# Linear attention followed by an MLP on one core: from two phases, one after the other, to one list-scheduled pipeline over batches

## The chip, the cores and the metric

The kernel runs on one core of one Trainium2 chip. The metric is device time in microseconds (us) of the slowest core, here the only one.

In the profile PE is TensorE's matmuls, PEld its weight loads, DVE is VectorE, ACT is ScalarE, POOL is GpSimd and SP is SyncE. L252 is line 252 of the kernel in question, so the same line number means something else in another kernel.

## The reference

```python
# q, k, v: (8 batches, 8 heads, 576 tokens, 64); omega: (128, 64)
def phi(x):                                   # on q and on k, both scaled by 64 ** -0.25
    h = einsum('bhsd,md->bhsm', x, omega) - sum(x * x, -1) / 2
    return exp(h - max(h, -1)) / sqrt(128)
q_p, k_p = phi(q_s), phi(k_s)
kv  = einsum('bhsm,bhsd->bhmd', k_p, v)
z   = sum(k_p, axis=2)
x   = (q_p @ kv) / (q_p @ z + 1e-6)           # attention, linear in the number of tokens
x   = x.transpose(0, 2, 1, 3).reshape(4608, 512)
h   = x @ w_in                                # (512, 2048)
out = (h * clip(h + 3, 0, 6) / 6) @ w_out     # (2048, 512), float32
```

Inputs and output are float32; both kernels multiply in bf16. Both drop the factors of a query token, which cancel in the quotient, and turn the maximum of a key token into a factor on its row of v.

## The kernel before

It works head by head, 64 heads, with 96 tokens on the partitions and six groups of them. Each engine has its program written out in order, with one semaphore for each kind of step. When all heads are done, the whole of x is transposed, and then the MLP runs.

```python
        def pe_T(g):                       # q and k of one head: transposes of 96 columns
            ...                            # waits for both casts, and for both exps of head g-2
            for r in range(NR):            # NR = 6
                ins = PE.transpose(rb[0:2 * D, CH * r:CH * r + CH], qkb[u][:, r, :, :]..., identb[0:CH, 0:CH])
        ...
        def pe_proj(g):
            PE.wait_ge(s_evq[u].h, g // 2 + 1)
            for i, (c0, c1) in enumerate(PQC):     # query: rows 0 to 63 of the array, 2 x 288 columns
                ins = PE.matmul(reg[0:M, c0:c1], omT[0:D, :], qkT[u][0:D, SH * i:SH * i + SH])
                if i == 1:
                    s_pq[u].inc(ins)
            for r in range(2, NR):                 # key: rows 64 to 127, 6 x 128 columns
                projk(r)
            PE.wait_ge(s_pq[u].h, g // 2 + 1)      # TensorE waits for its own query projection
            projk(0)
            s_pk[u].inc(projk(1))
        ...
        for t in range(NH + 5):            # NH = 64 heads
            dma_head(t + 2)
            pe_T(t); pe_kv(t - 2); pe_num(t - 3); pe_proj(t)
            act_expk(t - 1); act_expq(t - 1); act_kvc(t - 2); act_castk(t + 1)
            dve_div(t - 4); dve_evq(t); dve_rmax(t - 1); pool_castq(t + 1)   # runs on VectorE, despite its name
            pool_cmult(t - 1)
            ...                            # bounds of t, and the loads of the weights, cut
        for b in range(B):                 # all of x, transposed for the MLP
            for j in range(NJ):
                ...
        for tb in range(NBLK):             # 9 blocks of 512 tokens
            mm1_block(tb)                  # 16 x 4 matmuls of 512 columns; relu on ScalarE, min and product on VectorE
            ...
            if tb >= 1:
                mm2_block(tb - 1)          # 4 x 16 matmuls of 512 columns; copy on ScalarE; store
```

The softmax here doesn't subtract the row's maximum and nothing guards it: scores larger than these inputs give would overflow.

Of the kernel before, what the change touches and what calls it, by code (L numbers as in the profile page):

```python
# [12 lines left out]
class _Sem:  # L13
    __slots__ = ("h", "n")

    def __init__(self, h):
        self.h = h
        self.n = 0

    def inc(self, ins, d=1):  # L20
        ins.then_inc(self.h, d)
        self.n += d
        return ins
# [17 lines left out]
def _emit(nc, es, q, k, v, omega, w_in, w_out, out):  # L41
# [4 lines left out]
    NR = 6  # L46
    CH = S // NR
    assert S == CH * NR and CH <= 96 and S % 2 == 0, "kernel assumes seq = 6*CH, CH<=96"
    assert D == 64 and 96 <= M <= 128 and omega.shape[1] == D
    assert w_in.shape[0] == HID and w_out.shape[0] == DFF and w_out.shape[1] == HID  # L50
    NTOK = B * S
    assert out.shape[0] == NTOK and out.shape[1] == HID
    assert NTOK % 128 == 0 and HID % 128 == 0 and DFF % 128 == 0
    NJ = HID // 128
    NF = DFF // 128
    NH = B * H
    BLK = 512
    NBLK = (NTOK + BLK - 1) // BLK
    alpha = float(D) ** -0.25
    DE = D + 2  # L60
    SH = S // 2

    PE, ACT, DVE, POOL, SP = nc.tensor, nc.scalar, nc.vector, nc.gpsimd, nc.sync
# [4 lines left out]
    def pst(name, shape, dt):  # L68
        return es.enter_context(nc.psum_tensor(name, list(shape), dt))

    def sem(name):
        return _Sem(es.enter_context(nc.semaphore(name)))

    qk32 = [sbt("qk32_%d" % u, [CH, NR, 2, D], F32) for u in range(2)]
    qkb = [sbt("qkb%d" % u, [CH, NR, 2, D], BF16) for u in range(2)]
    vb = [sbt("vb%d" % u, [CH, NR, DE], F32) for u in range(4)]
    vc = [sbt("vc%d" % u, [CH, NR, DE], BF16) for u in range(2)]
    qkT = [sbt("qkT%d" % u, [2 * D, S], BF16) for u in range(2)]
    qpT = [sbt("qpT%d" % u, [M, S], BF16) for u in range(4)]
    kp = [sbt("kp%d" % u, [CH, NR, M], BF16) for u in range(2)]  # L80
    mx = [sbt("mx%d" % u, [CH, NR], F32) for u in range(2)]
    cc = [sbt("cc%d" % u, [CH, NR], F32) for u in range(2)]
    rec = [sbt("rec%d" % u, [CH, NR], F32) for u in range(2)]
    kvs = [sbt("kvs%d" % u, [M, DE], BF16) for u in range(2)]
    omT = sbt("omT", [2 * D, M], BF16)
    om32 = sbt("om32", [M, D], F32)
    omb = sbt("omb", [M, D], BF16)
    ident32 = sbt("ident32", [128, 128], F32)
    identb = sbt("identb", [128, 128], BF16)
    halfc = sbt("halfc", [128, 1], F32)  # L90
    xbufs = [sbt("xb%d" % bb, [CH, NR, HID], BF16) for bb in range(B)]
    xT = [sbt("xT%d" % j, [128, NTOK], BF16) for j in range(NJ)]
    w_in_bf = sbt("w_in_bf", [128, NJ, DFF], BF16)
    w_out_bf = sbt("w_out_bf", [128, NF, HID], BF16)
    gT = [sbt("gT%d" % u, [128, NF, BLK], BF16) for u in range(2)]
    NHP = 4
    tsb = [sbt("tsb%d" % u, [128, BLK], BF16) for u in range(NHP)]
    NTC = BLK // 128
    osb = [sbt("osb%d" % u, [128, NTC, HID], F32) for u in range(2)]

    P8 = pst("p8", [128, 4096], F32)
    regs = [P8[:, 0:1536], P8[:, 1536:3072]]
    regb = [r.bitcast(BF16) for r in regs]
    numbk = [P8[:, 3072:3584], P8[:, 3584:4096]]
    PQC = [(0, SH), (512, 512 + SH)]

    def pk_cols(r):
        if r == 0:
            return (SH, SH + M)
        if r == 1:  # L110
            return (512 + SH, 512 + SH + M)
        return (1024 + M * (r - 2), 1024 + M * (r - 1))

    s_qin = [sem("qin%d" % u) for u in range(2)]
    s_kin = [sem("kin%d" % u) for u in range(2)]
    s_vin = [sem("vin%d" % u) for u in range(4)]
    s_cq = [sem("cq%d" % u) for u in range(2)]
    s_ck = [sem("ck%d" % u) for u in range(2)]
    s_tt = [sem("tt%d" % u) for u in range(2)]
    s_evq = [sem("evq%d" % u) for u in range(2)]  # L120
    s_pq = [sem("pq%d" % u) for u in range(2)]
    s_pk = [sem("pk%d" % u) for u in range(2)]
    s_mx = [sem("mx%d" % u) for u in range(2)]
    s_rmx = [sem("rmx%d" % u) for u in range(2)]
    s_eq = [sem("eq%d" % u) for u in range(2)]
    s_ek = [sem("ek%d" % u) for u in range(2)]
    s_kv = [sem("kv%d" % u) for u in range(2)]
    s_kvc = [sem("kvc%d" % u) for u in range(2)]
    s_cm = [sem("cm%d" % u) for u in range(2)]
    s_num = [sem("num%d" % u) for u in range(2)]  # L130
    s_rec = [sem("rec%d" % u) for u in range(2)]
    s_div = [sem("div%d" % u) for u in range(2)]
    s_xtp = [sem("xtp%d" % u) for u in range(2)]
    s_xev = [sem("xev%d" % u) for u in range(2)]
    s_mm1 = [sem("mm1_%d" % u) for u in range(NHP)]
    s_hs1 = [sem("hs1_%d" % u) for u in range(NHP)]
    s_hs2 = [sem("hs2_%d" % u) for u in range(NHP)]
    s_mm2 = [sem("mm2_%d" % u) for u in range(2)]
    s_oev = [sem("oev%d" % u) for u in range(2)]
    s_c0 = sem("c0")  # L140
    s_idb = sem("idb")
    s_om = sem("omdma")
    s_omc = sem("omc")
    s_omt = sem("omt")
    s_oms = sem("oms")
    s_w = sem("wdma")
    s_out = [sem("odma%d" % u) for u in range(2)]

    blk = es.enter_context(nc.Block())

    @blk.sync
    def _body(_eng):
        s_c0.inc(POOL.memset(ident32[:], 0.0))
        POOL.wait_ge(s_c0.h, s_c0.n)
        s_c0.inc(POOL.affine_select(out=ident32[:], in_=ident32[:],
                                    compare_op=ALU.not_equal, fill=1.0, base=0,
                                    pattern=[[-1, 128]], channel_multiplier=1))
        c0_ident = s_c0.n
        s_c0.inc(POOL.memset(halfc[:], 0.5))
        c0_half = s_c0.n  # L160
        for u in range(4):
            s_c0.inc(POOL.memset(vb[u][:, :, :], 0.0))  # L162
        POOL.wait_ge(s_c0.h, s_c0.n)
        for u in range(4):
            s_c0.inc(POOL.memset(vb[u][:, :, D:D + 1], 1.0))
        c0_vb = s_c0.n
        POOL.wait_ge(s_c0.h, c0_ident)
        s_idb.inc(POOL.dma_start(identb[:], ident32[:]), 16)
        w_next = [0]
        NWP = NF + DFF // 128  # L170

        s_om.inc(SP.dma_start(om32[:], omega), 16)
        ACT.wait_ge(s_om.h, 16)
        s_omc.inc(ACT.copy(omb[:], om32[:]))
        PE.wait_ge(s_omc.h, 1)
        PE.wait_ge(s_idb.h, 16)
        PE.transpose(regb[0][0:D, 0:M], omb[:], identb[0:M, 0:M])
        s_omt.inc(PE.transpose(regb[0][D:2 * D, 0:M], omb[:], identb[0:M, 0:M]))
        ACT.wait_ge(s_omt.h, s_omt.n)
        s_oms.inc(ACT.copy(omT[:, :], regb[0][0:2 * D, 0:M]))  # L180

        def head_bh(g):
            return divmod(g, H)

        def dma_head(g):
            b, h = head_bh(g)
            u = g % 2
            if g < 2:
                SP.wait_ge(s_c0.h, c0_vb)
            if g >= 2:  # L190
                SP.wait_ge(s_cq[u].h, g // 2)
                SP.wait_ge(s_ck[u].h, g // 2)
            s_qin[u].inc(SP.dma_start(
                qk32[u][:, :, 0, :], q[b, h].rearrange("(r p) d -> p r d", p=CH)), 16)
            s_kin[u].inc(SP.dma_start(  # L195
                qk32[u][:, :, 1, :], k[b, h].rearrange("(r p) d -> p r d", p=CH)), 16)
            if g >= 4:
                SP.wait_ge(s_cm[u].h, g // 2 - 1)
            s_vin[g % 4].inc(SP.dma_start(
                vb[g % 4][:, :, 0:D], v[b, h].rearrange("(r p) d -> p r d", p=CH)), 16)  # L200

        def in_val(g):
            return 16 * (g // 2 + 1)

        def pool_castq(g):
            u = g % 2
            DVE.wait_ge(s_qin[u].h, in_val(g))
            if g >= 2:
                DVE.wait_ge(s_tt[u].h, g // 2)
            s_cq[u].inc(DVE.tensor_copy(qkb[u][:, :, 0, :], qk32[u][:, :, 0, :]))  # L210

        def act_castk(g):
            u = g % 2
            ACT.wait_ge(s_kin[u].h, in_val(g))
            if g >= 2:
                ACT.wait_ge(s_tt[u].h, g // 2)
            s_ck[u].inc(ACT.copy(qkb[u][:, :, 1, :], qk32[u][:, :, 1, :]))  # L217

        def pe_T(g):
            u = g % 2  # L220
            rb = regb[u]
# [132 lines left out]
        for t in range(NH + 5):  # L354
            if t + 2 < NH:
                dma_head(t + 2)
            if t < NH:
                pe_T(t)
# [187 lines left out]
```

## Time and profile before

| | before |
|---|---|
| time, median of 2 runs | 459.48 us (459.21 to 459.74) |
| attention, all heads | to 191 us (the last numerators; the prediction took 187) |
| transposes of x | from 192 to about 203 us |
| MLP | the remaining 254 us |
| busy, PE / DVE / ACT / POOL | 421.9 / 262.3 / 255.9 / 79.5 us |

The page of the profile and the main stretches are shown in the prediction. What it does not show are the groups of instructions on TensorE by shape, in this form: line, engine, operation, output<-inputs, shapes, count | busy us, mean ns of one | idle time before them and what ended it.

```profile
L252 PE MATMUL p<-omT,qkT 64*96 64x128 bf16 x384 | 70.5, 319 | 3.3
L333 PE MATMUL p<-kvs,qpT 128*96 128x66 bf16 x384 | 42.7, 268 | 0.0
L231 PE MATMUL p<-identb,qkb 96*128 96x96 bf16 x384 | 42.0, 277 | 10.8 <-issue 6.0 <-DVE qkb L210 3.9 <-ACT qkb L217 0.8
```

"64\*96" means that 64 rows and 96 columns of the array hold weights. None of these three attention groups has the 128\*128 of the MLP's. Their means of about 300 ns each overlap, so they are no rate: the transposes of L231 show a mean of 277 ns and start 80 ns apart. The rate is the distance from one start to the next, which is what I use below.

### The profile page before, as it was taken

The numbers are of one execution on the slowest core, as the hardware profiler recorded it, in microseconds if no ns is written. First come the engines' busy times: TensorE is split into PE (matmuls) and PEld (weight loads), VectorE is DVE, ScalarE is ACT, GpSimd is POOL, SyncE is SP. The second block draws the span as 40 slices with busy tenths as digits, with TensorE's granted clock in tenths as the row PEclk, the third lists the DMA queues.
The fourth block names the chain that finished last, engine by engine and source line by source line (L and its number), as shares of the span: only waits on it lengthen the run. The fifth ranks groups of instructions, "written<-read, shape, count | busy, mean of one in ns | idle before, by whom it ended". The sixth has DMA issues, their size and how long they took to land.

```text
span 457.8 us, 8404 instructions
## 1 busy us (share of the span) xinstructions
PE 421.9 (92%) x2986; PEld 251.4 (55%) x3010; DVE 262.3 (57%) x544; ACT 255.9 (56%) x519; POOL 79.5 (17%) x112
## 2 busy tenths in 40 slices
PE   2998889978999999699999999999999999999995
PEld 1676667766777777574444444444444444444442
DVE  1887888978989989667723608144170633607100
ACT  3766667766677677387735627254371734627221
POOL 2454446554333333200000000000000000000000
PEclk9999999999999999999999999999999999999999
DMA  6899999999677776000002002020100202002022
GB/s 125 184 200 197 197 191 196 207 196 202 157 162 170 177 161 152 3 1 1 0 1 92 1 7 85 1 92 1 74 19 0 92 2 92 1 0 92 1 92 92
DMA packets 129496, 42.55 MB, mean 93 GB/s; under 512 B 122800, under 2 KB 124848, under 8 KB 129456
## 3 DMA queue, kind: packets, MB, share of 16 engines
q1 hardware_dynamic: 118560, 37.79, 35.0%
q0 software_dynamic: 10896, 4.23, 8.1%
q8 instruction: 24, 0.39, 0.4%
q14 instruction: 16, 0.13, 0.1%
HBM read 36.73 MB, written 9.44 MB: 101 GB/s over the span
## 4 chain that ended last, share of the span: by engine, by line
PE 55%; issue 23%; POOL 17%; ACT 2%; DMA 1%; POOLq 1%; DVE 0%; SPq 0%
PE p L495 27%; PE p L457 27%; POOL vc L306 12%; POOL w_in_bf L389 3%; POOL w_out_bf L385 2%; ACT xT L428 1%; PE p L420 1%; DMA vb<-in_v_dram 1%; POOLq L305 1%; POOL vb L162 0%; DVE xb L348 0%; POOLq L38 0%; ACT osb L501 0%; SPq L195 0%; PE p L333 0%
## 5 line engine op out<-in xcount | busy, mean ns | idle before, releaser
L470 DVE SCALAR_TENSOR_TENSOR gT<-tsb,p 128x512 bf16<-128x512 bf16 x144 | 99.0, 687 | 124.1 <-ACT tsb L466 123.4
L457 PE MATMUL p<-xT,w_in_bf 128*128 128x512 bf16 x564 | 124.8, 379 | 1.7 <-ACT xT L428 1.1
L495 PE MATMUL p<-w_out_bf,gT 128*128 128x512 bf16 x564 | 125.0, 379 | 0.6
L466 ACT ACTIVATE tsb<-p,halfc 128x512 bf16<-128x512 f32 x144 | 98.9, 687 | 27.1 <-PE p L457 27.0
L457 PEld LDWEIGHTS p<-xT,w_in_bf 128*128 128x128 bf16 x576 | 56.2, 98 | 68.8 <-issue 1.0
L495 PEld LDWEIGHTS p<-w_out_bf,gT 128*128 128x128 bf16 x576 | 56.4, 98 | 67.9
L501 ACT COPY osb<-p 128x512 f32<-128x512 f32 x36 | 21.1, 585 | 102.4 <-PE p L495 102.4
L306 POOL TENSOR_TENSOR vc<-vb,cc 96x396 bf16<-96x396 f32 x64 | 55.4, 866 | 109.3 <-DVE cc L296 109.3
L252 PE MATMUL p<-omT,qkT 64*96 64x128 bf16 x384 | 70.5, 319 | 3.3
L292 DVE TENSOR_REDUCE mx<-kp 96x6 f32<-96x768 bf16 x64 | 60.1, 938 | 0.9 <-ACT kp L287 0.9
L252 PEld LDWEIGHTS p<-omT,qkT 64*96 64x96 bf16 x384 | 43.4, 181 | 17.0 <-PE p L256 17.0
L231 PE MATMUL p<-identb,qkb 96*128 96x96 bf16 x384 | 42.0, 277 | 10.8 <-issue 6.0
L217 ACT CAST qkb<-qk 96x384 bf16<-96x384 f32 x64 | 33.3, 520 | 23.2 <-DMA qk<-in_k_dram 22.8
L256 PE MATMUL p<-qkT,omT 64*128 64x288 bf16 x128 | 42.0, 431 | 1.1 <-DVE qkT L244 1.1
L333 PE MATMUL p<-kvs,qpT 128*96 128x66 bf16 x384 | 42.7, 268 | 0.0
L286 ACT ACTIVATE kp<-p 96x256 bf16<-96x256 f32 x64 | 24.2, 378 | 32.8 <-PE p L252 32.7
L244 DVE COPY qkT<-p 128x576 bf16<-128x576 bf16 x64 | 29.3, 457 | 21.6 <-PE p L231 19.8
L275 ACT ACTIVATE qpT<-p 128x576 bf16<-128x576 f32 x64 | 41.4, 646 | 0.0
L231 PEld LDWEIGHTS p<-identb,qkb 96*128 96x128 bf16 x384 | 29.0, 133 | 20.8 <-DVE qkb L210 7.8
L333 PEld LDWEIGHTS p<-kvs,qpT 128*96 128x96 bf16 x384 | 37.6, 194 | 0.0
L287 ACT ACTIVATE kp<-p 96x512 bf16<-96x512 f32 x64 | 37.3, 584 | 0.0
L315 PE MATMUL p<-vc,kp 96*128 96x66 bf16 x384 | 31.7, 240 | 5.6 <-POOL vc L306 2.2
(30 smaller groups left out, 192.7 us busy)
## 6 DMA issues: line engine op xcount, KB each, us to landing
qk<-in_q_dram SPq DMA_DIRECT2D x64, 144.0 KB, 3.1
qk<-in_k_dram SPq DMA_DIRECT2D x64, 144.0 KB, 3.8
vb<-in_v_dram SPq DMA_DIRECT2D x64, 144.0 KB, 4.1
out_dram<-osb SPq DMA_DIRECT2D x9, 1024.0 KB, 4.3
w_out_bf<-in_moe_w_out_dram POOLq DMA_DIRECT2D x16, 128.0 KB, 4.4
w_in_bf<-in_moe_w_in_dram POOLq DMA_DIRECT2D x16, 128.0 KB, 5.1
om<-in_omega_dram SPq DMA_DIRECT2D x1, 32.0 KB, 1.8
identb<-ident POOLq DMA_DIRECT2D x1, 32.0 KB, 2.8
```

Source lines behind the costliest of these rows:

```text
L231: ins = PE.transpose(rb[0:2 * D, c0:c1], qkb[u][:, r, :, :].rearrange("p t d -> p (t d)"), identb[0:CH, 0:CH])
L252: return PE.matmul(reg[0:CH, c0k:c1k], qkT[u][D:2 * D, CH * r:CH * r + CH], omT[D:2 * D, :])
L256: ins = PE.matmul(reg[0:M, c0:c1], omT[0:D, :], qkT[u][0:D, SH * i:SH * i + SH])
L275: s_eq[u].inc(ACT.activation(dst, src, AF.Exp, scale=alpha))
L287: s_ek[u].inc(ACT.activation(kp[u][:, 2:6, :], srcB, AF.Exp, scale=alpha))
L292: s_mx[u].inc(DVE.reduce_max(mx[u][:], kp[u][:], axis=AX.X))
L306: s_cm[u].inc(POOL.tensor_tensor(vc[u][:], vb[g % 4][:], ccb[u], ALU.mult))
L333: ins = PE.matmul(numbk[u][0:CH, DE + DE * r:2 * DE + DE * r], qpT[q4][:, CH * r:CH * r + CH], kvs[u][:])
L457: ins = PE.matmul(hps[par][:, 0:T], w_in_bf[:, c, 128 * f:128 * f + 128], xT[c][:, tok0:tok0 + T], start=(c == 0), stop=(c == NJ - 1))
L466: s_hs1[par].inc(ACT.activation(tsb[par][:, 0:T], hps[par][:, 0:T], AF.Relu, bias=halfc[:, :], scale=1.0 / 6.0))
L470: s_hs2[par].inc(DVE.scalar_tensor_tensor(gT[ub][:, f, 0:T], tsb[par][:, 0:T], 1.0, hps[par][:, 0:T], ALU.min, ALU.mult))
L495: last = PE.matmul(ops[par][0:128, 0:HID], gT[ub][:, f, 128 * tc:128 * tc + 128], w_out_bf[:, f, :], start=(f == 0), stop=(f == NF - 1))
```

## The change

The intent is to let TensorE work on the MLP while the other engines prepare the next batch's attention, and to make TensorE's attention work cheaper in itself.

- A small scheduler takes every operation with what it reads and writes, an assumed duration and a priority. It plays them through on a model of the engines and fixes the order of each. Priorities place the attention of batch b+1 beside the MLP of batch b.
- Two heads share 128 partitions, 64 each. One partition holds nine consecutive tokens of a head, so a row of q, k or v is 2304 B in one piece.
- The projections use all 128 rows, with a weight matrix half filled with zeros. A kv product does two heads at once.
- The first token of each nine goes into a ninth block of 512 tokens at the end.
- The casts of q and k are GpSimd's. The transposes are matmuls against an identity.

```diff
-        for t in range(NH + 5):
-            pe_T(t); pe_kv(t - 2); pe_num(t - 3); pe_proj(t)
-        ...                      # then the transposes of x, then
-        for tb in range(NBLK):
-            mm1_block(tb)
-            if tb >= 1:
-                mm2_block(tb - 1)
+    for b in range(B):
+        attention(b)             # operations with priorities near b - 1
+        if b == 0:
+            continue
+        blk = b - 1
+        for f in range(NF):
+            mm1(blk, f)          # priority blk + f / 16
+            if blk >= 1 and f % 4 == 0:
+                mm2(blk - 1, f // 4)
+    for blk in (7, 8, 9):
+        ...                      # the last blocks, without attention
+    G.schedule()
-            s_qin[u].inc(SP.dma_start(
-                qk32[u][:, :, 0, :], q[b, h].rearrange("(r p) d -> p r d", p=CH)), 16)
+            for which, src, key in ((0, q, "q32"), (1, k, "k32")):
+                op("SP", 1.0, lambda E, ...: E.dma_start(
+                    qk32[u3][:, which, :], src[b, 2 * pr:2 * pr + 2].rearrange("h (p r) d -> (h p) (r d)", r=NR)), ...)
+            for which, key in ((0, "q32"), (1, "k32")):
+                op("POOL", 0.65, lambda E, ...: E.tensor_copy(
+                    qkb[u2][:, :, which, :], qk32[u3][:, which, :]...), ...)
-                ins = PE.matmul(reg[0:M, c0:c1], omT[0:D, :], qkT[u][0:D, SH * i:SH * i + SH])
+                return E.matmul(ring.t[vQ.slot], omq[:], qkT_r.t[vqk.slot][:]..., start=True, stop=True)
-                return PE.matmul(reg[0:CH, c0k:c1k],
-                                 qkT[u][D:2 * D, CH * r:CH * r + CH], omT[D:2 * D, :])
+                for i in range(4):
+                    ins = E.matmul(ring.t[vK.slot][:, 128 * i:128 * i + 128], qkT_r.t[vqk.slot][:, i, :], omk[:],
+                                   start=True, stop=True)
```

(The scheduler itself and the other operations are cut.)

## The prediction

The prediction and the expectations call two rates cold and warm. They are the two that the distances between starts show in the trace of the kernel before: 80 ns for 96 columns (L231) and 106 or 107 for 128 (L252), 1.2 columns per ns; and 216 ns for 512 (L457, L495), 2.4 columns per ns. That the rebuilt attention would run at the second was my estimate, and so are the 56 ns for 128 columns and 57 for 130, a little above the 54 and 55 that 512 in 216 gives.

> **What bounds the kernel now.** I read the page first: busy shares, the 40 slices, the chain that ended last.
>
> ```profile
> span 457.8 us, 8404 instructions
> ...
> PE 421.9 (92%) x2986; PEld 251.4 (55%) x3010; DVE 262.3 (57%) x544; ACT 255.9 (56%) x519; POOL 79.5 (17%) x112
> ...
> PE   2998889978999999699999999999999999999995
> ...
> DMA  6899999999677776000002002020100202002022
> ...
> PE 55%; issue 23%; POOL 17%; ACT 2%; DMA 1%; POOLq 1%; DVE 0%; SPq 0%
> ```
>
> The slices show two programs laid end to end. For the first 16 slices DMA works and PE is mixed; then DMA stops and PE runs alone. The chain is the MLP's matmuls for 54% and, in the first part, issue and GpSimd in turn. A sum over stretches gives each part its length:
>
> ```profile
> 12.00:180.00 168.00, 152.04 (x1550) 119.28 (x1548) 144.44 (x357) 116.54 (x301) 72.89 (x92) 1.00 0.98 184
> 180.00:187.00 7.00, 6.37 (x64) 4.80 (x62) 6.12 (x16) 4.24 (x14) 2.59 (x3) 1.00 0.22 49
> 187.00:200.00 13.00, 10.05 (x162) 9.88 (x163) 7.57 (x18) 7.05 (x15) 0.84 (x1) 1.00 0.01 4
> 200.00:230.00 30.00, 28.80 (x185) 14.58 (x185) 22.58 (x36) 23.73 (x37) 0.00 (x0) 1.00 0.00 1
> 230.00:458.00 228.00, 221.31 (x1010) 100.63 (x1029) 79.28 (x116) 99.78 (x151) 0.00 (x0) 1.00 0.11 42
> ```
>
> The columns are length, busy us of PE, its weight loads, DVE, ACT and POOL, granted clock, DMA share and GB/s. Attention fills the time to about 187 us, the transposes that turn its output for the MLP to about 203, the MLP the remaining 254. In attention PE is "busy" nine tenths and DMA 98% at only 184 GB/s; in the MLP every other engine has room. A busy PE may still be slow, so I took spacings from the chain in order of time:
>
> ```profile
> 192.40 4.48 PE p L420 x54
> ...
> 203.83 10.74 PE p L457 x49
> ```
>
> 54 transposes of 96 columns in 4.48 us are 83 ns each; 49 matmuls of 512 columns in 10.74 us are 219 ns each. The MLP streams 2.3 columns per ns, the transposes 1.2: half.
>
> [...]The granted clock of 1.00 in all stretches doesn't show this state, the spacing does. [...]loads of 64x96 (L252) average 181 ns, of 128x128 98 ns. [...]here 122800 of 129496 packets are under 512 B, and the DMA is at 98% for 184 GB/s.
>
> **The change, part by part.** The list order of each engine in the changed program (no time is in it) gives the counts.
>
> *MLP matmuls, unchanged:* 1152 of 512 columns x 216 ns = 249 us. They are 54% of the span now, and can't shrink.
>
> *Attention on PE, rebuilt.* Before, 26 matmuls per head, 2712 columns: 2.26 us at the cold rate, 1.2 us at the warm one; a head takes (187-12)/64, about 2.7 us. After, two heads share 128 partitions, every weight load has 128 columns, no tile of 64 rows is left, and MLP matmuls lie between, so I take the warm rate. 288 transposes of 128 columns and 288 key projections of 128, each 56 ns: 32.3. 72 query projections of 512 x 216 ns: 15.6. 288 kv of 130 x 57: 16.4. 320 numerators of 65 columns: [...]each brings a new weight load, so I choose 50: 16. 128 output transposes x 56: 7.2, 32 small ones: 1.5. Sum **89 us**, instead of about 200 us of attention and transposes.
>
> So PE needs 249 + 89 = **338 us** if it never waits. Attention isn't hidden behind the MLP on PE; what is hidden is its waiting[...].
>
> *ACT.* 144 relu: before 687 ns each with a bias read from a tile; the exp of 512 without one takes 584 (L287). The new bias is a constant, I take 600: 86 us. 144 exps of 512 x 584: 84. 91 copies of 512 x 585: 53. Sum 224 us, 66% of 338.
>
> *DVE.* 144 scalar_tensor_tensor x 687 ns: 99. 72 maxima of 512, by 938 ns x 512/768, about 650: 47. 64 reciprocals x 187: 12. 32 divisions of 640 elements, from 554 ns at 384[...], about 820: 26. 49 copies of 512 at about 650: 32, 37 smaller ones: 11. Sum 227 us, 67%.
>
> *POOL.* It now casts q and k: 64 x 576 elements at about 0.9 us (estimate: the two-input L306 takes 866 ns for 396, a memset of 396 takes 419, so one input lies between): 58. 64 products of 576 elements, 866 x 576/396 less the fixed part, 1.25: 80. 64 small copies and 8 weight loads: 18. The emitter makes each POOL operation wait for the one before, some 0.1 us each: 20. Sum 176 us, half.
>
> *DMA.* Rows of nine tokens make packets of 2304 B instead of 256 B. 36.7 MB read and 9.4 written over 370 us are 125 GB/s, below the 184 to 207 that it reached with small packets. Not a bound, except at the start.
>
> *Start.* Nothing of the MLP can run before batch 0 has passed through attention. The first q lands about 4 us in, as before (first cast at 5.88). POOL's order until the last product of batch 0 holds 11 casts, 4 weight issues, 8 products with small copies: 11 + 3.6 + 12.4 = 27 us with the waits, so about 31 to 33; then kv, copy, numerators, reciprocal, division, transpose, copy, some 5 us. First MLP matmul at about **35 us**. By then PE has done attention of batch 0 (89/8 = 11 us) and about three of nine units of batch 1 (2 us).
>
> *Sum.* 35 + (338 - 13) + 3 for the last copy and store = 363 us. In between I allow 3% of waits, 10 us: the order is fixed in advance with assumed durations close to those measured (512-element copy: assumed 0.53 plus 0.1, measured 0.585 plus its signal), so some operations will be late, but one hidden tile takes PE 338/144 = 2.35 us with all that lies between, so each of the two h banks has 2 x 2.35 - 0.86 = 3.8 us between its matmuls, and the relu and product on it need some 1.5. That is 373 of span; before, the time is 1.7 above the span, so **375 us**, a gain of 18%.
>
> **The rivals.**
> 1. *Waits eat the overlap.* PE is in order, and an attention matmul placed too early blocks ready MLP matmuls behind it. Some 30 such points per batch at 0.3 us make 9 us of 41, over 70 us in all: 435. For it: four PSUM banks in a ring, one nearly always held by the MLP output, and two for h. Against: ACT and DVE have a third of their time free, and every wait on PE gives them time to catch up, so it doesn't add up fully. I give 10% to 395 and above.
> 2. *The POOL chain becomes the bound.* It would need its 22 us per batch to rise above 42, so casts of 2.5 us or more. No row of the trace shows such a cast; the products are known. It would show at the start first: +8 us for casts of 1.7 us.
> 3. *The array stays cold in the attention parts.* The 89 us would become about 150 and the time 435.[...]
> 4. *Fewer waits than assumed*, start at 28 us, small matmuls at 40 ns: 355.
>
> **Range and chances.** The sum's floor is 338 + 15 of start and end, 353. Above, a start 8 us later and 7% of waits make 398. I say 357 to 397 for 8 in 10; slower than before would need 95 us of waits, which nothing speaks for. Faster 0.98, same 0.01, slower 0.01.
>
> **What would show each step right or wrong.** The MLP groups should keep spacings of 216 ns, attention matmuls of 128 columns 56 to 60, and no group with PE loads near 180 ns should be left. PE's spacing sum should be near 338. First MLP matmul at 30 to 38 us; POOL nearly solid until then, with casts of about 0.9 us. In the steady part one batch every 40 us, ACT and DVE at 60 to 70%, DMA far below nine tenths. The chain should be PE's by more than 80%, with POOL only at its start. The prediction is wrong if PE's idle time after 40 us is over 25 us, if a copy, an exp or a product by DVE is far longer than before[...], if the casts on POOL are twice my guess[...].

## The result and the profile after

The changed kernel takes **363.83 us** (363.66 and 363.99); before it was 459.48. Ratios here and below are the mean time of one kernel's runs over the mean time of the other's runs of the same rounds, so they are not quite the ratio of the medians quoted. This one is 0.7918, with a 95% interval of 0.7895 to 0.7941.

The page of the changed kernel, the lines that answer to those of before (span, busy times, slices of PE and DMA, shares of the chain that ended last):

```profile
span 361.9 us, 6522 instructions
...
PE 342.1 (95%) x2569; PEld 189.3 (52%) x2569; DVE 222.0 (61%) x406; ACT 211.2 (58%) x383; POOL 137.4 (38%) x206
...
PE   3677998999999999999999999999999999999994
...
DMA  7999699635234531645155513322110121121123
...
PE 80%; POOL 11%; DVE 3%; ACT 2%; issue 1%; DMA 1%; SPq 0%; POOLq 0%
```

There is one program now, not two. TensorE fills from about the eighth slice to the end, and the DMA's share is above 1.0 only at the start (1.03 at 297 GB/s in the first 36 us). The same kernel by stretches (length, then busy us of PE, PEld, DVE, ACT and POOL with their counts, granted clock, DMA share, GB/s):

```profile
0.00:36.00 36.00, 22.71 (x228) 16.41 (x229) 21.89 (x47) 20.06 (x38) 26.50 (x44) 0.91 1.03 297
36.00:60.00 24.00, 23.25 (x204) 13.70 (x202) 21.69 (x40) 19.56 (x40) 18.39 (x27) 1.00 0.89 213
60.00:80.00 20.00, 19.13 (x147) 10.32 (x146) 13.16 (x25) 11.68 (x21) 7.72 (x12) 1.00 0.53 143
80.00:120.00 40.00, 40.00 (x335) 22.99 (x333) 28.50 (x54) 24.28 (x45) 16.75 (x25) 1.00 0.45 124
120.00:200.00 80.00, 79.88 (x638) 45.04 (x636) 53.22 (x99) 54.32 (x100) 35.05 (x51) 1.00 0.43 123
200.00:320.00 120.00, 119.82 (x855) 64.13 (x854) 71.15 (x127) 70.61 (x126) 33.01 (x50) 1.00 0.22 56
```

From 80 to 320 us, 239.7 of 240 us have TensorE busy, while VectorE and ScalarE are at some 60 to 70%. Three microseconds from there show how (start us, us busy, then the group):

```profile
150.02 0.39 PE L416 MATMUL p<-omk,qkT 128*128 128x128 bf16 x4
150.25 0.38 PE L411 MATMUL p<-qkT,omq 128*128 128x512 bf16 x1
150.46 1.03 PE L556 MATMUL p<-wo,gT 128*128 128x512 bf16 x4
151.32 0.47 PE L488 MATMUL p<-kvz,qpT 128*128 128x65 bf16 x10
151.64 0.39 PE L401 MATMUL p<-ident,qkb 128*128 128x128 bf16 x4
151.86 1.03 PE L532 MATMUL p<-xT,wi 128*128 128x512 bf16 x4
```

Key projections, a query projection, a piece of the second MLP product, the numerators of a pair of heads, transposes of the next tokens, a piece of the first MLP product: a part of attention lies between every two groups of the MLP. From start to start, four matmuls of 128 columns take 0.22 to 0.23 us, four of 512 take 0.86, and ten of 65 columns take 0.32. None of these groups shows a wait ahead of it.

Taking every group's count times its usual start-to-start spacing, the columns come to 81.5 us for attention (transposes 16.1, keys 16.1, queries 15.5, kv 16.3, numerators 9.5, output transposes 7.1 and 0.9) and 248.4 us for the MLP, 330 together. The rest of the 361.9 us is 2.8 before the first matmul, 19.3 of gaps and slow spacing before the first MLP matmul at 35.9 us, 4.8 in all the rest, and about 5 after the last matmul has started. (I count 57 ns for a kv matmul and 30 for a numerator; the usual spacing in the trace is 59 for the first and 29 to 35 for the second, which would move about a microsecond from the gaps to the columns.)

### The profile page after: what moved, and what is told of

The parts are those of the page before. It is cut to its first block, busy times and chain, and to the rows that moved or that the text cites. A ratio compares the mean times of both kernels' runs of the same rounds, so it can differ in the third digit from the quotient of the medians.

```text
span 361.9 us, 6522 instructions
## 1 busy us (share of the span) xinstructions
PE 342.1 (95%) x2569; PEld 189.3 (52%) x2569; DVE 222.0 (61%) x406; ACT 211.2 (58%) x383; POOL 137.4 (38%) x206
## 4 chain that ended last, share of the span: by engine, by line
PE 80%; POOL 11%; DVE 3%; ACT 2%; issue 1%; DMA 1%; SPq 0%; POOLq 0%
PE p L556 32%; PE p L532 30%; POOL vbd L462 7%; PE p L473 4%; PE p L416 4%; PE p L401 4%; PE p L411 3%; PE p L488 2%; POOL qkb L379 2%; PE p L507 1%; DVE mx L429 1%; ACT kp L422 1%; POOL vbd L465 1%; DMA qk<-in_k_dram 1%; ACT qpT L425 1%
## 5 line engine op out<-in xcount | busy, mean ns | idle before, releaser
L556 PE MATMUL p<-wo,gT 128*128 128x512 bf16 x576 | 145.2, 379 | 0.5 <-ACT kp L422 0.5
L537 ACT ACTIVATE tsb<-p 128x512 bf16<-128x512 f32 x144 | 86.3, 599 | 89.3 <-PE p L532 89.1
L532 PE MATMUL p<-xT,wi 128*128 128x512 bf16 x512 | 130.4, 379 | 0.1
L462 POOL TENSOR_TENSOR vbd<-v,cc 64x576 bf16<-64x576 f32 x64 | 73.7, 1152 | 45.0 <-DVE cc L457 30.6
L556 PEld LDWEIGHTS p<-wo,gT 128*128 128x128 bf16 x576 | 54.6, 98 | 57.6 <-ACT kp L422 0.7
L379 POOL CAST qkb<-qk 128x576 bf16<-128x576 f32 x64 | 42.7, 668 | 87.7 <-PE p L401 80.1
L532 PEld LDWEIGHTS p<-xT,wi 128*128 128x128 bf16 x512 | 47.1, 98 | 45.0 <-DVE gT L539 0.9
L429 DVE TENSOR_REDUCE mx<-kp 128x4 f32<-128x512 bf16 x72 | 49.0, 681 | 8.4 <-ACT kp L422 8.0
L422 ACT ACTIVATE kp<-p 128x512 bf16<-128x512 f32 x72 | 43.0, 598 | 12.7 <-PE p L416 11.9
L425 ACT ACTIVATE qpT<-p 128x512 bf16<-128x512 f32 x72 | 43.1, 599 | 1.0 <-PE p L411 0.3
```

The lines of the kernel that those rows point to most:

```text
L379: op("POOL", 0.65, lambda E, which=which, u3=u3, u2=u2: E.tensor_copy(qkb[u2][:, :, which, :], qk32[u3][:, which, :].rearrange("p (r d) -> ...
L422: op("ACT", actt(512), lambda E, u=u, vK=vK: E.activation(kp[pb][:, 4 * u:4 * u + 4, :].rearrange("p c m -> p (c m)"), ring.t[vK.slot], AF ...
L425: op("ACT", actt(512), lambda E, u=u, vQ=vQ: E.activation(qpT[pb][:, :, 4 * u:4 * u + 4, :].rearrange("m h c p -> m c h p"), ring.t[vQ.slo ...
L429: op("DVE", dvet(512), lambda E, u=u: E.reduce_max(mx[pb][:, 4 * u:4 * u + 4], kp[pb][:, 4 * u:4 * u + 4, :], axis=AX.X), pos(u) + 0.03, r ...
L462: op("POOL", 1.3, lambda E, p0=p0, p1=p1, f0=f0, cbc=cbc: E.tensor_tensor(vbd[u2][p0:p1, :, f0:f0 + 64], v32[u3][p0:p1, :, :], cbc, ALU.mu ...
L532: ins = E.matmul(h_ps[hu], wi[:, c, 128 * f:128 * f + 128], xv[:, c, :], start=(c == 0), stop=(c == NJ - 1))
```

## The experiments

### 1. The rebuilt attention alone, without the interleaving (a_serial)

Each matmul of the first MLP product also waits for the last result of attention of all batches. xT gets eight buffers instead of two, so that all of x can be kept.

```diff
+    xT = [sbt("xT%d" % u, [128, NJ, 512], BF16) for u in range(8)]
-            xk = [("xT", blk % 2, j) for j in range(NJ)]
+            xk = [("xT", blk, j) for j in range(NJ)] + [("xS", b) for b in range(B)]
-        if b == 0:
-            continue
+    for b in range(1, B):
```

> The changed kernel with all eight batches of attention first and the whole MLP after it (eight transposed-output buffers instead of two; same instructions, same list scheduling). Theory (interleaving and the rebuilt attention each carry part of the gain): the MLP alone keeps 249 + about 10 us; attention alone has POOL 137, ACT and DVE about 125 us busy and 81 us of TensorE columns at the warm rate, 163 at the cold one, so it takes 150 (warm) to 185 us (cold) and the kernel 405 to 445 us. If the spacing of its 128-column matmuls goes to 107 ns the array was cold, if it stays 56 it was warm. Rival A (the rebuilt attention is the whole gain, the interleaving only hides what was hidden anyway): 365 to 380. Rival B (the rebuilt attention is worth nothing by itself): 455 or more.

Measured: 427.66 us, ratio to before 0.9297 (0.9267 to 0.9326). The first MLP matmul starts at 169.2 us, against 203.8 before. Slices of PE and POOL on the page:

```profile
PE   3667777678768785999999999999999999999995
...
POOL 4997997899898974000000000000000000000000
```

The rebuilt attention by itself takes 32 us off (459.5 to 427.7) and the interleaving another 64 (427.7 to 363.8). Without the interleaving, attention's 81.5 us of columns stretch over 169 us: some 88 us of TensorE's time are lost to waits and slow spacing. GpSimd is the busiest engine there, 137 of the 169 us (VectorE has 126), and 19 of the 45 us in which the profile shows TensorE waiting end on GpSimd. That looks like rival 2 of the prediction, hidden by the interleaving; no run makes GpSimd faster, so it is not shown that GpSimd alone holds this phase.

### 2. Is TensorE's column time the bound? (a_pe_extra)

Each of the 144 tiles of the first MLP product gets one more matmul of 512 columns, whose result is overwritten. Nothing else changes.

```diff
         def e(E):
+            E.matmul(h_ps[hu], wi[:, 0, 128 * f:128 * f + 128], xv[:, 0, :], start=True, stop=True)
             for c in range(NJ):
```

> The changed kernel with one 512-column matmul more per hidden tile of the MLP (144 in all, result overwritten by the group that follows), order unchanged. Theory (TensorE never waits once the MLP has begun, so its column sum is the time): 144 x 216 ns = 31.1 us more, 394 to 396. Rival (waits on other engines have slack in them that the added matmuls fill): 15 us or less, under 380.

Measured: 393.26 us, ratio 0.855. The addition is 144 x 216 ns = 31.1 us of columns and the kernel became 29.4 us longer. A microsecond added to TensorE is nearly a microsecond of the kernel, so TensorE is the bound.

### 3. How much of ScalarE's slack is free? (a_act_extra)

Each relu runs twice, once into a scratch tile.

```diff
+        def e_relu(E):
+            E.activation(scr[tu][:], h_ps[hu], AF.Relu, bias=0.5, scale=1.0 / 6.0)
+            return E.activation(tsb[tu][:], h_ps[hu], AF.Relu, bias=0.5, scale=1.0 / 6.0)
```

> The changed kernel with every relu on ACT done twice (the first result is thrown away), order unchanged: ACT has 144 x about 0.5 us = 72 us more to do, from 211 to about 283 us busy, and each h bank is held 0.5 us longer. Theory (TensorE is the bound and ACT's third of idle time is real slack): 364 to 372. Rival (the order is so tight that the other engines' time shows through): most of the 72 us comes on top, 400 or more.

Measured: 376.18 us, ratio 0.8205, a little above what was expected. Busy times of this kernel's page:

```profile
PE 343.9 (92%) x2521; PEld 186.9 (50%) x2569; DVE 221.3 (59%) x406; ACT 273.9 (73%) x527; POOL 137.2 (37%) x206
```

ScalarE worked 63 us more (211.2 to 273.9) and the kernel became 12.4 us longer: about a fifth leaks through. Slack on an engine off the path was not wholly free here. Two reasons are at hand: the order was fixed for shorter durations, and each relu holds its PSUM bank longer before the next matmuls may write it. No run separates them.

### 4. What are the long rows worth? (a_rows256)

The tiles for q, k and v are laid out so that a row's nine tokens land apart, which makes packets of 256 B again; all else is as after.

```diff
-                    qk32[u3][:, which, :], src[b, 2 * pr:2 * pr + 2].rearrange("h (p r) d -> (h p) (r d)", r=NR)),
+                    qk32[u3][:, :, which, :], src[b, 2 * pr:2 * pr + 2].rearrange("h (p r) d -> (h p) r d", r=NR)),
...                              # v32 likewise, by a row of 66 instead of 64
```

> The changed kernel with q, k and v landing in buffers whose rows are broken up, so that DMA packets are 256 B again as in the kernel before; same order of instructions on all compute engines. Theory (DMA bounds at most the start): 28 MB in small packets at the 195 GB/s of the kernel before still fit into 362 us, only the first batches come later: first MLP matmul 6 to 12 us later, time 369 to 377. Rival (large packets are what freed the attention): the steady part is held up too, 395 or more.

Measured: 376.77 us, ratio 0.8189. First the rates of the changed kernel's page, for comparison, then those of this one (GB/s by slice):

```profile
GB/s 254 346 279 309 158 223 240 200 95 161 72 94 127 168 115 37 187 130 159 31 145 175 161 29 99 92 55 70 31 29 2 31 58 29 31 54 33 31 60 85
```

```profile
GB/s 165 198 189 194 205 207 206 185 218 211 206 61 81 144 149 119 65 151 158 120 45 170 139 140 32 120 63 90 31 28 30 28 30 56 30 28 56 30 52 88
```

Small packets stop at 165 to 218 GB/s, and the first MLP matmul slips from 35.9 to 45.7 us. From 80 us on, both kernels have TensorE solid. The long rows are worth 13 us, all of it before 80 us.

### 5. What does a tile of 64 rows cost? (a_tile64)

The two projections use their 64 rows alone, as before; everything else stays.

```diff
-                return E.matmul(ring.t[vQ.slot], omq[:], qkT_r.t[vqk.slot][:]..., ...)
+                return E.matmul(ring.t[vQ.slot], omq[0:64, :], qkT_r.t[vqk.slot][0:64]..., ...)
-                    ... qkT_r.t[vqk.slot][:, i, :], omk[:], ...
+                    ... qkT_r.t[vqk.slot][64:128, i, :], omk[64:128, :], ...
```

> The changed kernel with the query and key projections back on 64 rows of the array (partitions 0 to 63 and 64 to 127, contraction 64) instead of 128 rows with zero weights; same columns, same order. Theory ([...]full height is worth something): 144 changes each way, each some 0.1 us, time 372 to 385, and the matmul that follows a change starts over 0.1 us later than its columns say. Rival (it costs nothing, full height is neutral): 362 to 366.

Measured: 366.31 us, ratio 0.7963 (0.7943 to 0.7983) against 0.7918: slower by 2.5 us, and the larger expectation missed. PE in order of time, where the tiles of 64 rows stand between groups on the whole array:

```profile
151.09 0.69 PE L473 MATMUL p<-vbd,kp 128*128 128x130 bf16 x9
151.71 0.23 PE L416 MATMUL p<-omk,qkT 64*128 64x128 bf16 x1
151.72 0.39 PE L411 MATMUL p<-qkT,omq 64*128 64x512 bf16 x1
151.78 0.33 PE L416 MATMUL p<-omk,qkT 64*128 64x128 bf16 x3
152.04 1.04 PE L556 MATMUL p<-wo,gT 128*128 128x512 bf16 x4
```

The cost of changing the tiling is there. A 512-column matmul is followed after 311 ns by a 64-row one, where 216 is usual, and a 64-row one by a whole-array one after 155 instead of 56. That is about 97 ns each way, 144 changes, 14 us. But the query matmul on the upper 64 rows and the key matmuls on the lower 64 run at the same time: the key matmul that starts after the query's comes 52 or 53 ns later, not 216. That gives back nearly all of it.

### 6. What sets the start? (a_start, a_start2)

In a_start the scheduler may give batch 0's casts to VectorE and ScalarE too, and its products and small copies to VectorE.

```diff
-                op("POOL", 0.65, ...
+                op("POOL" if b > 0 else ("POOL", "DVE", "ACT"), {"POOL": 0.65, "DVE": 0.45, "ACT": actt(576)}, ...
-            op("POOL", 1.3, ...
+            op("POOL" if b > 0 else ("DVE", "POOL"), {"POOL": 1.3, "DVE": dvet(576)}, ...
```

> The changed kernel with the casts of q and k and the products of v of batch 0 alone allowed on DVE and ACT as well, chosen by the list scheduler; later batches as before. Theory (the 22 us that TensorE idles before the first MLP matmul are held by the chain of products and casts on POOL): first MLP matmul at 26 to 30 instead of 35.9 us, time 354 to 359. Rival (the start is held by the loads, 293 GB/s at full DMA, or by ACT): first MLP matmul at 34 or later, time 361 to 365.

Measured: 363.44 us, ratio 0.79 (0.7879 to 0.7921), no difference. The first MLP matmul came at 35.7 us, so the theory missed. VectorE in order of time, two products of the same shape:

```profile
14.05 0.76 DVE L463 TENSOR_TENSOR vbd<-v,cc 64x576 bf16<-64x576 f32 x1
...
16.61 2.31 DVE L463 TENSOR_TENSOR vbd<-v,cc 64x576 bf16<-64x576 f32 x1
```

and GpSimd in the same stretch:

```profile
14.06 0.83 POOL L466 CAST vbd<-cc 64x9 bf16<-64x9 f32 x1
...
17.12 1.17 POOL L463 TENSOR_TENSOR vbd<-v,cc 64x576 bf16<-64x576 f32 x1
```

The product took 2.31 us while GpSimd had a product of its own in hand, and 0.76 when it had only a nine-column copy; that copy took 0.83 us instead of the usual 0.22. Here the two engines held each other up. VectorE took three of batch 0's eight products, and one of them lost time in this way; that this alone ate the gain is not shown.

In a_start2 batch 0's work goes first on GpSimd, ahead of any cast of batch 1, with four buffers for the casts instead of three, its loads assumed faster by the scheduler, and batch 0's small copies go to ScalarE.

```diff
-                   t0 - 0.05, reads=[(key, u3)], writes=[("qkb", u2, which)], lat=0.15)
+                   t0 - 0.05, reads=[(key, u3)] + (["b0"] if b == 1 else []), writes=[("qkb", u2, which)], lat=0.15)
...                              # "b0" is written by batch 0's last products
```

> The changed kernel with POOL's work of batch 0 put in better order: four cast buffers instead of three and loads of batch 0 assumed faster, so that all casts of batch 0 come ahead of its products; the small copies of batch 0 on ACT; casts of batch 1 only after the last product of batch 0. No engine gets products that it does not have now (giving them to DVE did not help: a DVE product took 2.3 us while POOL read too). Theory (the order on POOL holds the start): first MLP matmul at 29 to 32 instead of 35.9 us, time 357 to 361. Rival (the start is the length of one batch's chain through all engines, or work put off for batch 1 comes back as waits at 50 to 80 us): 362 to 366.

Measured over five rounds: 363.95 us, ratio 0.7915 (0.7891 to 0.7938). The first MLP matmul did come at 31.6 us, 4.3 earlier. In stretches:

```profile
0.00:36.00 36.00, 23.60 (x230) 15.15 (x231) 23.57 (x49) 21.65 (x45) 23.69 (x34) 1.00 1.03 305
36.00:60.00 24.00, 21.11 (x205) 12.77 (x203) 18.78 (x38) 18.04 (x36) 19.34 (x28) 1.00 0.95 217
```

TensorE is busier before 36 us (23.6 against 22.7) and less busy from 36 to 60 (21.1 against 23.3). What was put off, batch 1's attention, came back as waits, and the last matmul starts at 356.9 us in both kernels. So GpSimd's order does set when the first MLP matmul comes, but the kernel's time does not follow it. My reading is that the time hangs on how much attention of the first two batches must be got through; which engine limits that is not shown. A rival is the DMA: its share is 1.03 to 36 us in both kernels, and slower loads (experiment 4) put the first MLP matmul off by 10 us.

### 7. What held a head before? (b_rows, b_fill, b_rows_fill)

Before, a head took 2.71 us in the second half of attention and 2.94 in the first (from the first numerators of heads 32 and 57, and of heads 8 and 32). Candidates were the DMA with its small packets, the array at half rate, and chains of waits. In b_rows, q and k come in rows of 1536 B (v stays at 256 B); the order of tokens is put right when x is copied after its transposes. In b_fill, four matmuls of 512 columns without use go ahead of a head's transposes, to see whether TensorE then leaves the half rate. b_rows_fill does both.

```diff
 # b_rows
-                qk32[u][:, :, 0, :], q[b, h].rearrange("(r p) d -> p r d", p=CH)), 16)
+                qk32[u][:, 0, :, :], q[b, h].rearrange("(p r) d -> p r d", p=CH)), 16)
-                dst = xT[j][:, S * b:S * b + S]
+                dst = xT[j][:, S * b:S * b + S].rearrange("n (p r) -> n r p", r=NR)
 # b_fill, in pe_T, after its waits
+            if g >= 2:
+                for _ in range(4):
+                    PE.matmul(regs[u][:, 0:512], omT[:, :], qkT[u][:, 0:512], start=True, stop=True)
```

> The kernel before with q and k loaded in rows of six tokens (1536 B a packet instead of 256 B; v stays at 256 B); the token order is put right in the copies that fill the MLP's input. It asks what held the attention stage of the kernel before. Theory (TensorE at the cold rate, 80 ns for 96 columns, holds a head at 2.6 us; the DMA at 98% is second and only just): 445 to 460. Rival (the DMA held it): a head at 1.7 to 2.0 us, 64 heads save 40 us or more, 420 or less.

> The kernel before with four more 512-column matmuls per head from the third head on, written to PSUM columns that the transposes overwrite next (62 x 4 = 248 matmuls whose result is thrown away; outputs unchanged). Theory[...]: spacing of the 96-column transposes goes from 80 to 42 ns, a head is 1.2 + 0.86 us of columns plus waits, and the time is 430 to 470 in spite of 53 us (warm) of added work. Rival[...]: 248 x 427 ns = 106 us more, 550 to 570. Second rival (warm, but the DMA holds a head at 2.6 us anyway): 455 to 465, which the run with both changes tells apart.

> The kernel before with both: packets of 1536 B for q and k, and four 512-column matmuls per head thrown in. Theory[...]: a head falls to 2.1 to 2.4 us and the time to 420 to 445, below each change alone. Rival (chains of waits between engines hold a head[...]): 455 or more.

Measured: b_rows 476.44 us, ratio 1.0391. The last numerator came at 185.1 us, against 191.0, a head in the first half took 2.73 us instead of 2.94, and in the second half 2.69 instead of 2.71. So the small packets held the first half, and they cost 6 us. The total is slower for a reason of the experiment's own. The copies that restore the order, by groups:

```profile
engine op xcount: duration ns min/median/max, first and last start us, forms
L428 ACT COPY xT<-p x16: 2086/2318/2325, 187.2 to 215.7; 128x576 bf16<-128x576 bf16 x16
```

and the same line before:

```profile
L428 ACT COPY xT<-p x16: 638/678/778, 193.1 to 202.7; 128x576 bf16<-128x576 bf16 x16
```

Writing bf16 elements 12 bytes apart made ScalarE's copy more than three times as long (2318 ns against 678), and VectorE's, of the same shape, almost five times (L431: a mean of 2213 against 457). That confound makes the total of b_rows useless; its attention part can be read.

b_fill took 485.2 us (ratio 1.0581) and b_rows_fill 508.47 (1.1085). b_rows and b_fill lie outside every range that was expected; b_rows_fill lies in its rival's (455 or more), but the slow copies of b_rows are in it too. In both, most transposes of 96 columns stand 41 to 47 ns apart instead of 80: with four more matmuls a head the half rate was gone. Yet a head took 3.2 us in both. TensorE and VectorE of b_fill in order of time:

```profile
150.67 1.04 PE L231 MATMUL p<-qkT,omT 128*128 128x512 bf16 x4 [0.54 <-DVE qkb L210]
151.55 0.42 PE L234 MATMUL p<-identb,qkb 96*128 96x96 bf16 x6
```

```profile
150.29 0.33 DVE L210 CAST qkb<-qk 96x384 bf16<-96x384 f32 x1
...
152.00 0.46 DVE L247 COPY qkT<-p 128x576 bf16<-128x576 bf16 x1 [0.70 <-PE p L234]
152.38 0.94 DVE L295 TENSOR_REDUCE mx<-kp 96x6 f32<-96x768 bf16 x1
153.35 0.19 DVE L299 RECIPROCAL cc<-mx 96x6 f32<-96x6 f32 x1
```

The filler waits for VectorE's cast of q; the transposes stand behind the filler; VectorE's copy waits for the transposes; the maximum, the reciprocal and the next cast stand behind that copy in VectorE's order. With the filler in it, this circle is 3.2 us long. The experiment ended the half rate and closed a new loop at the same time, so it says nothing about how long a head would take at the full rate.

### 8. VectorE and ScalarE as holders of a head before (b_castpool, b_shortexp)

b_castpool moves the cast of q from VectorE to GpSimd, which also opens the circle of experiment 7.

```diff
-            s_cq[u].inc(DVE.tensor_copy(qkb[u][:, :, 0, :], qk32[u][:, :, 0, :]))
+            s_cq[u].inc(POOL.tensor_copy(qkb[u][:, :, 0, :], qk32[u][:, :, 0, :]))
```

b_shortexp adds to this that each exponential does about a quarter of its columns (the rest of the tiles holds constants). Its output is wrong, which doesn't matter for the time.

```diff
-            s_eq[u].inc(ACT.activation(dst, src, AF.Exp, scale=alpha))
+            s_eq[u].inc(ACT.activation(dst[:, :, 0:72], src[:, :, 0:72], AF.Exp, scale=alpha))
...                              # the key's two exponentials likewise: 32 of 128 columns
```

> The kernel before with the cast of q moved from DVE to POOL (which is at 32% in attention); nothing else. The runs with thrown-in matmuls showed a warm array and longer heads[...]. New theory: DVE and its round trip to TensorE hold it. DVE's six instructions of a head sum to 2.65 us, and the next head's transposes wait for the cast of q, the last of them but two. Without it DVE has 2.3 us and the round trip loses the cast: a head at 2.3 to 2.45 instead of 2.7 us, time 435 to 448. Rival (the cold array's 2.26 us of columns and its waits, or the DMA at 98%, hold a head at 2.6 anyway): 454 to 462.

> Wrong result on purpose. The kernel before with the cast of q on GpSimd (as in b_castpool, 457.9 us, a head every 2.65 us in the middle of attention, VectorE at some 2.3 us per head), and with each exponential cut to about a quarter of its columns, the rest of the tiles filled once with constants. That takes ScalarE's three exponentials of a head from 1.61 us to about 0.75. Theory A, the loop of each of the two PSUM regions (transposes, copy, projections, exponentials, and only then the transposes two heads later) holds a head at 2.65 us: the loop shrinks by some 0.85 us per two heads, a head comes to about 2.2 to 2.35, attention ends 15 to 25 us earlier, total 433 to 443. Theory B, TensorE's columns at the cold rate (2.26 us) with its small waits, or the DMA, hold it: a head stays at 2.5 to 2.65 us and the total at 450 to 458.

Measured: b_castpool 457.88 us, ratio 0.9952 (0.9921 to 0.9983), with VectorE's busy time down from 262.3 to 242.6 us; a head in the second half takes 2.654 us instead of 2.705. It missed the expected 435 to 448 and lies in its rival's range. b_shortexp took 460.12 us, ratio 1.0015 (0.9987 to 1.0043), with ScalarE's busy time down from 255.4 to 209.3 us; a head takes 2.654 us again, the same to a nanosecond. Theory A of the last run falls. Theory B's figure for a head came, its total was missed by 2 us (the first numerator comes 3.3 us later than in b_castpool, behind added memsets), and its reason is not what the trace shows. First the waits of TensorE that the profile counts in 60 us of b_shortexp (engine, line, released by: us in total, times, longest):

```profile
PE p L235 <- POOL qkb L214: 1.3, 2, 0.7
PE p L235 <- issue: 1.2, 1, 1.2
```

That is 2.5 us of 60, as if TensorE alone set the pace. But a wait counts there only after TensorE's modelled busy time has run out: six transposes are drawn 0.66 us long, though the last of them starts after 0.40. The distances between starts show more. In 51 of the 56 heads from 32 to 59 of b_castpool and b_shortexp, the first kv matmul starts 0.10 us after GpSimd's product for that head ends. In every second head that is some 380 ns after the last transpose, where 80 is the least. GpSimd's product in turn ends a row of steps; here is one round of b_castpool, other lines left out:

```profile
140.15 0.46 DVE L244 COPY qkT<-p 128x576 bf16<-128x576 bf16 x1 [0.31 <-PE p L231]
...
140.53 0.94 DVE L292 TENSOR_REDUCE mx<-kp 96x6 f32<-96x768 bf16 x1
...
141.50 0.19 DVE L296 RECIPROCAL cc<-mx 96x6 f32<-96x6 f32 x1
...
141.77 0.85 POOL L306 TENSOR_TENSOR vc<-vb,cc 96x396 bf16<-96x396 f32 x1 [1.21 <-DVE cc L296]
...
142.71 0.49 PE L315 MATMUL p<-vc,kp 96*128 96x66 bf16 x6
...
144.71 0.66 PE L231 MATMUL p<-identb,qkb 96*128 96x96 bf16 x6
...
145.41 0.46 DVE L244 COPY qkT<-p 128x576 bf16<-128x576 bf16 x1 [0.31 <-PE p L231]
```

VectorE copies the transposes of one head, then takes the maximum of the head before and its reciprocal; GpSimd's product follows; then TensorE does the kv product, the numerators, the projections and the transposes two heads on, and VectorE copies those. The round is 5.26 us for two heads, 2.63 a head. Its steps take the same time in b_shortexp to some 10 ns, because neither change touches them. In the kernel before the round is 5.31 us and closes through VectorE alone: in 26 of the 28 heads from 32 to 59 the kv product starts 0.147 us after VectorE's division, which stood behind the cast of q. b_castpool took the cast out of this row, but the branch over GpSimd's product is only some 0.03 us a head shorter, so little was gained. In the second half of attention, then, a loop between TensorE and VectorE, with GpSimd just behind, sets the pace; TensorE's part is 2.7 of the 5.3 us, at half rate. The copy stands ahead of the maximum only by the order on VectorE. No run shortens both branches, so the loop is read from the traces and not tested.

Within TensorE's part, spacings that recur in each head show what it spends beyond its columns: 201 ns from the last numerator to the first query projection, where 80 is usual between numerators; about 240 from the last key projection to the first transpose, where 106 is usual between key projections; and 362 instead of 106 before the last two key projections, where the kernel makes TensorE wait for its own query projection (`PE.wait_ge(s_pq...)`). The first two stand where the tiling changes, and are of the size that experiment 5 found (97 ns there, some 120 and 135 here, at half rate). The changed kernel has none of the three.

## Why the prediction was right

The mechanism held, and the sum lay 11 us above the measured time. By its own steps:

- **Columns on TensorE: predicted 338, found 330.** The MLP was right to half a microsecond. The step that was mis-sized is the numerators: I chose 50 ns for a matmul of 65 columns with new weights, which made 16 us; they stand 29 to 35 ns apart, 9.5 to 10 us. The 50 was a guess. At 29 ns next to nothing of the load of 128 columns of weights shows: 65 columns at the MLP's 512 in 216 ns would take 27 (estimate). Before, 66-column numerators with 96 columns of weights stood 80 ns apart, where 66-column kv matmuls with 128 columns of weights stood 54; what makes that difference is not shown.
- **The bound.** Said to be TensorE with 66 to 67% on ScalarE and VectorE. Experiment 2 confirms it: 31.1 us more of columns, 29.4 us more of time.
- **Waits in the steady part: allowed 10, found 4.8 after 35.9 us**, most of them before 80. Rival 1 did not come about. Experiment 3 shows how near it is: one engine with 63 us more work costs 12.
- **The start: predicted 35, found 35.9, partly for wrong reasons.** GpSimd's casts take 0.67 us, not 0.9, its products 1.15, not 1.25, and its sum is 137 us, not 176. The chain of waits shows batch 0's last product on GpSimd ending at about 29.6 us, earlier than the 31 to 33 of the prediction; then 6.3 us passed where 5 were allowed. GpSimd was not nearly solid until then either, but busy for 22.3 of the first 30 us. So errors that partly cancel made the number. Experiment 6 shows that GpSimd's order does move the first MLP matmul, by 4.3 us, as the prediction had it; what failed is that the start enters the sum one for one: the time did not change.
- **The end: allowed 3, about 5.**

The differences close the sum: 373 less 8 of columns, less 5 of waits, plus 1 at the start and 2 at the end is 363, against a span of 361.9; the columns and spacings that I count are good to about a microsecond.

- **The rate of attention doubled.** Shown by spacings: 128 columns 107 ns apart before, 56 after, so rival 3 did not come about. The granted clock is 1.00 in nearly all of both, and does not show it. What kept attention at half rate before is only narrowed down: with four more 512-column matmuls a head it ends (b_fill, 41 to 47 ns for 96 columns instead of 80). It also ends within the transposes of x of the kernel before, with nothing but transposes on TensorE: almost all of the first 54 stand 80 ns apart, and the rest, from 4.3 us after the first on, 42 to 43. The rebuilt attention alone (a_serial) already runs mostly at 56 ns, with lapses, so the MLP between is not needed for it.
- **"What is hidden is its waiting."** Shown by experiment 1: run alone, the rebuilt attention loses 88 us of TensorE's time; the interleaving takes 64 us off the kernel.

The 200 us of attention and transposes before had been explained by TensorE at half rate and by a DMA at 98%. Each holds for one half, the first in part. In the first half the small packets held a head at 2.94 us. In the second, at 2.65 to 2.71, the loop of experiment 8 did: TensorE at half rate is half of it, and VectorE and the hand-overs are the rest. The prediction knew the 2.26 us of columns, but not this loop, nor the wait of TensorE for itself, nor the size of the changes of tiling.

**Open.** No run brings the kernel before to the full rate without closing another loop, and none opens the loop that holds a head there, so what a head would have taken at that rate is not known. The prediction gave no split of its 84 us of gain between the rebuilt attention and the interleaving; only experiment 1 does, and in that order only.

## What to carry to other kernels

When two phases have different bounds, lay one between the pieces of the other on the engine that both need. The limits of the shorter phase (here most likely GpSimd, 137 us of work in a phase of 169) can then vanish behind the longer one's columns, as they did here, and the estimate is the sum of columns plus the start and the end. Read the pace of TensorE from the distance between starts, not from its busy share, its counted waits or the granted clock: waits of 0.3 us were hidden there, and the granted clock was 1.00 at both rates. Look for waits of TensorE on itself, too. And before a filler or a detour is used to test one limit, follow what stands behind it in every engine's order: three of the runs here were spoilt by what the experiment itself had added.
